# Long convolution and SwiGLU block: two LN2 norms offered to VectorE, more warming products, a new listed order

## The chip, the cores and the metric

The kernel runs on one core of a Trainium2 chip. The metric is the device time of one launch in microseconds (us). The kernel before took 261.85 us, the median of three runs (261.59 to 262.32).

## The reference

`S` = 2048 rows, `D` = 640 columns, `F` = 1728, inputs in bf16, batch 1. LayerNorm has no weights. The causal convolution over the whole sequence is written as a product of Fourier transforms padded to 2S.

```python
kv   = shift_conv(k, shift_k) * v              # four taps along the rows
y    = irfft2(rfft2(pad(kv)) * rfft2(pad(ssm_k)))[:S] + kv * ssm_D
h    = q + layernorm(q) * y
n    = layernorm(h)
out  = h + (silu(n @ w_gate) * (n @ w_up)) @ w_down
```

## The kernel before

**Tiling.** The sequence is cut into four blocks of 512 rows (four tiles of 128). The long convolution goes by blocks too: each block of `kv` (spectrum X) and of `ssm_k` (G, and H for the windows made of two neighbouring G) is taken to the frequency domain by products with a constant matrix on TensorE (L387, evicted in L376), X and H are multiplied and summed on VectorE (`mac`, L776 to L819, mostly L788, L816 and L817), and `inverse` goes back by products on TensorE (L955). `inverse` starts with an odd half (L898) and a low half (L901, or a DMA add in L906's place), needs the normalised rows of `ln1` (ScalarE, L882), multiplies them with the result (L979), adds them into h (L993, or a DMA that adds, issued by POOL in L291), takes the squares' sums for LN2 (ScalarE, L828) and ends with LN2's norm. `turn_h` normalises h (L882 on ScalarE, L879 on VectorE) and transposes it: block 0 on TensorE (L1015), the others by DMAs on SP's queue (L1008, four of them). The FFN of a block follows: products with gate and up weights (L1179, stretches of five), evictions (L1169, L1171, L1190), the product of the two (VectorE, L1173), and products with w_down (L1072), whose sums are added to h and stored (L1116, L1118 and L1120 for the last rows). Stages are named by block: X1, G2, m12, i1, t1, f1 and so on.

**norm.** `norm` turns the sums of a row into mean and 1/deviation, on 128x4 numbers. On VectorE it is ten short instructions that end in a cubic polynomial (L847 to L858, L864); on POOL it uses a power (L860 to L862). `ln1` gives its norm to POOL for all four blocks. LN2's norm goes to POOL in blocks 1 and 2 (`LN2POOL`) and to VectorE in blocks 0 and 3.

**The order.** The kernel doesn't issue in program order. `Plan` first collects all operations with their engine, reads and writes; `ORDER` (L76 to L115) then lists them by number, 940 entries, and each engine and each DMA queue runs what it is given in that order, first in, first out. An operation can have an alternative on another engine (an eviction on VectorE instead of ScalarE, an addition as a DMA, a load on POOL's queue instead of SP's); a negative number in the list selects it. Tiles come from a few pools of fixed size (`SLOTS`: four in PSUM, twelve big ones in SBUF, eight for spectra, five rows), so that an order also sets which buffer an operation waits for.

**The start.** While the first loads are under way TensorE runs products of ones with ones (`spin`, L1323 to L1331, `WARMUP` = 18, 16 and 16 of them) whose results nobody reads. Between them stand the transposes of the taps (`turn_taps`, L1336, and `turn_pairs`, L1353). The first real work is the transposes of block 0 of ssm_k (L485, loaded in L342) and of k (L628, loaded in L615), then the product for `kv` (L660). L1434 loads the last rows of w_down, 80 KB, twice.

Of the kernel before, what the change touches and what calls it, by code (L numbers as in the profile page):

```python
# [17 lines left out]
D = 640  # L18
# [30 lines left out]
ADDINV = ()  # L49
WHOLE3 = False  # L50
WARMUP = (18, 16, 16)
MERGE = ()
WIDE = ()
H1ACT = ()
# [19 lines left out]
TW = PAD + BLK  # L74
CUTS = ("X0", "G0", "m", "i")
ORDER = [  # L76
# [39 lines left out]
SLOTS = {'S': 8, 'big': 12, 'kT': 0, 'tT': 1, 'row': 5, 'sg': 0, 'co': 2, 'ps': 4, 'sm': 6}  # L116
HOME = {t: "big" for t in ("scr", "x", "ld", "t4", "hT", "wgu", "diag")} | {"o": "row", "ps_c": "ps", "ps_f": "ps"}
SPLIT = ((0,), (1,))
# [101 lines left out]
def kernel(ctx: ExitStack, tc: tile.TileContext, A_q, A_k, A_v, A_shift_k, A_ssm_k, A_ssm_D, B_x,  # L220
# [28 lines left out]
    def ap(b):  # L249
        if b.tag != "big":  # L250
            return b.ap if b.tag is None else place[b.tag][b.at]
        t = place["big"][b.at]
        return t if b.kind == "ld" else t.rearrange("p (k n) -> p k n", k=KT if b.kind in ("hT", "wgu") else 4 * KT if b.kind == "diag" else R)

    def pe(ns, fn, r, w, holds=(), late=338):
        op = plan.add("pe", ns, fn, r, w, holds)
        op.late = late
        return op
# [571 lines left out]

    def norm(s, v, mean=None, bias=False, rs=range(R)):

        def fused(out, a, scalar, b, op0, op1):
            if v is nc.vector:
                v.scalar_tensor_tensor(out, a, scalar, b, op0=op0, op1=op1)
            else:
                v.tensor_scalar(out, a, scalar, None, op0=op0)
                v.tensor_tensor(out, out, b, op=op1)
# [3 lines left out]
        def sm(s, i):  # L842
            return ap(s)[:, i, rs[0]:rs[-1] + 1:rs[1] - rs[0]]

        def go():
            if mean and plan_block in MERGEH:
                v.tensor_scalar(sm(s, 2), sm(s, 0), -1.0 / D, None, op0=ALU.mult)  # L847
            elif mean:
                fused(sm(s, 2), sm(s, 0), -1.0 / D, sm(mean, 2), ALU.mult, ALU.add)
            v.tensor_mul(sm(s, 6), sm(s, 2), sm(s, 2))  # L850
            if v is nc.vector:
                fused(sm(s, 3), sm(s, 1), EPS, sm(s, 6), ALU.add, ALU.subtract)
                v.tensor_scalar(sm(s, 4).bitcast(I32), sm(s, 3).bitcast(I32), -0.5, float(0x5F165000), op0=ALU.mult, op1=ALU.add)
                v.tensor_mul(sm(s, 6), sm(s, 4), sm(s, 4))
                v.scalar_tensor_tensor(sm(s, 6), sm(s, 6), -1.0, sm(s, 3), op0=ALU.mult, op1=ALU.mult)
# [6 lines left out]
                v.tensor_tensor(sm(s, 4), sm(s, 3), ap(root)[:, rs[0]:rs[-1] + 1:rs[1] - rs[0]], op=ALU.pow)  # L862
            if bias:
                v.tensor_mul(sm(s, 5), sm(s, 2), sm(s, 4))  # L864
        plan.add("dve" if v is nc.vector else "pool", 2190 if v is nc.vector else 7000 if mean else 5500, go, ([mean] if mean else []) + ([root] if v is nc.gpsimd else []), [s])

    def ln1(x):
        s = new("sm")
# [442 lines left out]
    def first(name):  # L1311
        plan.line(0, name)
# [33 lines left out]
    if TWOTAPS:  # L1346
# [4 lines left out]
        def turn_pairs():  # L1351
            for t in range(4):
                nc.tensor.matmul(ap(pt2)[:, 0, t * KT:(t + 1) * KT], ap(by_pair)[0:KT, t * P:(t + 1) * P], ap(ident)[0:KT, 0:KT], start=True, stop=True)  # L1353
        plan.name = "k0"
        pe(150, turn_pairs, [(by_pair, 0), ident], [pt2], (), 258)
        plan.name = "load"
        act(200, lambda: nc.scalar.copy(ap(taps2), ap(pt2)[:, 0, 0:4 * KT]), [pt2], [taps2])
        plan.add("pool", 350, lambda: nc.gpsimd.tensor_tensor(ap(by_pair)[:, 4 * P:4 * P + H2], ap(ident)[:, 0:H2], ap(ident)[:, H2:P], op=ALU.add), [ident], [(by_pair, 1)])
# [37 lines left out]
            ap(minus)[:, 2:4, :].rearrange("p a (c q) -> p a c q", c=4), ap(WI)[:, :, 1::2].rearrange("p c a q -> p a c q"), -1.0, None, op0=ALU.mult))  # L1396

    first("k0")
    k = turned_k(k, spun, table)
    again = spun  # L1400
    if not K0TURN:
# [116 lines left out]
```

## Time and profile before

| | before |
|---|---|
| median of 3 runs | 261.85 us |
| the profiled execution | 263.34 us |
| its span | 261.6 us |
| TensorE busy | 248.9 us, 95% |
| VectorE busy | 197.1 us, 75% |
| ScalarE busy | 184.9 us, 71% |
| POOL busy | 99.4 us, 38% |
| granted TensorE clock | 1.0 |

The span reaches from the first to the last instruction of the profiled execution; its own time, 263.34 us, is measured around it. In the profile PE is TensorE's products and PEld its weight loads, DVE is VectorE, ACT ScalarE, POOL GpSimd, SP SyncE; a q behind the name is the engine's queue of DMA issues and waits. A row of the timeline gives start, duration, engine, line, operation, output and inputs, and in square brackets the idle time ahead of it and what ended it.

### The profile page before, as it was taken

What the parts mean: (1) busy time and instruction counts of PE and PEld (TensorE: products, weight loads), DVE (VectorE), ACT (ScalarE), POOL (GpSimd) and SP (SyncE); (2) the same over time, 40 slices, a digit from 0 to 9 for tenths busy, and PEclk for the clock granted to TensorE, in tenths of its full rate; (3) what the DMA queues carried; (4) which work ended last, traced back from release to release, by engine and by line L of the source; (5) the groups of instructions that cost most, each with busy time, mean ns of one, the idle gap of its engine ahead of it and who ended that gap; (6) DMA issues with size and microseconds to landing.
All of it is one profiled execution on the core that took longest, in us unless ns stands there. A gap on an engine that the chain in (4) does not pass through costs nothing.

```text
span 261.6 us, 4550 instructions
## 1 busy us (share of the span) xinstructions
PE 248.9 (95%) x1738; PEld 149.6 (57%) x1738; DVE 197.1 (75%) x251; ACT 184.9 (71%) x308; POOL 99.4 (38%) x114
## 2 busy tenths in 40 slices
PE   7999998799997979999999999999999999999993
PEld 7985675554464437664456476544446754444662
DVE  4499999999996979999899999999999200102222
ACT  2799999999968789689679874866596332474300
POOL 7390700019995290144919621246960023000000
PEclk9999999999999999999999999999999999999999
DMA  6969999976938999699978959999996447000011
GB/s 213 386 126 263 252 291 338 202 220 122 345 89 158 195 190 259 118 168 221 296 123 136 338 128 171 174 238 199 207 285 189 82 93 97 6 0 3 0 34 66
DMA packets 65278, 45.91 MB, mean 175 GB/s; under 512 B 31029, under 2 KB 60410, under 8 KB 65258
## 3 DMA queue, kind: packets, MB, share of 16 engines
q1 hardware_dynamic: 59152, 32.51, 50.4%
q0 software_dynamic: 6096, 13.12, 26.7%
q8 instruction: 13, 0.21, 0.4%
q14 instruction: 7, 0.06, 0.1%
q10 hardware_dynamic: 10, 0.01, 0.0%
HBM read 29.56 MB, written 4.59 MB: 131 GB/s over the span
## 4 chain that ended last, share of the span: by engine, by line
PE 67%; ACT 9%; DVE 8%; POOL 7%; DMA 5%; issue 2%; DVEq 0%; POOLq 0%
PE ps L1179 31%; PE ps L1072 23%; POOL sm L850 6%; PE ps L387 5%; DMA big<-row 3%; PE ps L955 2%; ACT row L882 2%; DMA big<-in_A_ssm_k_dram 2%; PE ps L660 2%; ACT S L376 1%; DVE big L969 1%; ACT big L487 1%; ACT big L376 1%; DVE big L788 1%; DVE S L534 1%
## 5 line engine op out<-in xcount | busy, mean ns | idle before, releaser
L1179 PE MATMUL ps<-big,big 128*128 128x512 bf16 x540 | 119.8, 379 | 0.6 <-ACT co L1190 0.6
L1179 PEld LDWEIGHTS <-big 128*128 128x128 bf16 x540 | 52.6, 98 | 61.5 <-issue 1.1
L1072 PE MATMUL ps<-wd,tT 128*128 128x320 bf16 (+2 forms) x416 | 59.2, 299 | 0.5 <-ACT tT L1171 0.5
L1072 PEld LDWEIGHTS <-tT 128*128 128x128 bf16 x416 | 40.3, 98 | 17.7 <-issue 2.0
L1173 DVE TENSOR_TENSOR tT<-tT,co 128x2048 bf16<-128x2048 bf16 x12 | 14.7, 1223 | 38.9 <-ACT tT L1171 20.8
L387 PE MATMUL ps<-big,WF 128*128 128x320 bf16 x224 | 37.3, 298 | 2.7 <-ACT co L1169 1.2
L1169 ACT CAST co<-ps 128x1024 bf16<-128x1024 f32 x24 | 23.9, 1009 | 18.7 <-PE ps L1179 18.6
L816 DVE TENSOR_TENSOR big<-S,S 128x2560 bf16<-128x2560 bf16 x24 | 34.8, 1487 | 0.2
L817 DVE TENSOR_TENSOR S<-S,big 128x2560 bf16<-128x2560 bf16 x21 | 30.8, 1488 | 0.1
L387 PEld LDWEIGHTS <-WF 128*128 128x128 bf16 x224 | 21.3, 97 | 14.1 <-issue 4.9
L1171 ACT ACTIVATE tT<-ps 128x1024 bf16<-128x1024 f32 x24 | 24.3, 1027 | 3.8 <-PE ps L1179 3.5
L828 ACT ACTIVATE row<-big 128x640 bf16<-128x640 bf16 x32 | 23.5, 738 | 4.2 <-DMA big<-row 2.3
L1108 POOL DMA_DIRECT2D out_dram<-row x12 | 12.0, 1156 | 36.3 <-ACT row L1107 36.3
L882 ACT ACTIVATE row<-big,sm 128x640 bf16<-128x640 bf16 x23 | 19.7, 914 | 3.7 <-POOL sm L864 2.2
L850 POOL TENSOR_TENSOR sm<-sm 128x4 f32<-128x4 f32 x6 | 19.9, 3318 | 5.2 <-ACT row L871 5.0
L376 ACT CAST S<-ps 128x640 bf16<-128x640 f32 (+1 forms) x28 | 15.6, 613 | 2.0 <-PE ps L387 2.0
L376 ACT ACTIVATE big<-ps 128x640 bf16<-128x640 f32 (+1 forms) x27 | 15.5, 629 | 1.3 <-PE ps L387 1.1
L1107 ACT CAST row<-ps 128x640 bf16<-128x640 f32 x12 | 7.7, 700 | 10.8 <-PE ps L1072 10.8
L291 POOL DMA_DIRECT2D S<-big x6 | 7.2, 1206 | 19.0 <-DVE big L816 5.9
L955 PEld LDWEIGHTS <-WI 128*128 128x128 bf16 x96 | 9.4, 98 | 6.7 <-issue 1.7
L1050 POOL DMA_DIRECT2D big<-in_B_w_gate_dram x8 | 8.7, 1219 | 9.4 <-issue 6.8
L788 DVE TENSOR_TENSOR S<-S,S 128x2560 bf16<-128x2560 bf16 (+1 forms) x10 | 12.2, 1219 | 0.0
(112 smaller groups left out, 320.9 us busy)
## 6 DMA issues: line engine op xcount, KB each, us to landing
big<-in_B_w_up_dram SPq DMA_DIRECT2D x18, 320.0 KB, 5.6
big<-in_B_w_gate_dram SPq DMA_DIRECT2D x16, 320.0 KB, 5.5
big<-in_A_ssm_k_dram SPq DMA_DIRECT2D x4, 640.0 KB, 6.7
big<-in_A_q_dram SPq DMA_DIRECT2D x4, 640.0 KB, 5.5
big<-in_A_v_dram SPq DMA_DIRECT2D x4, 640.0 KB, 7.7
S<-big POOLq DMA_DIRECT2D x4, 640.0 KB, 6.3
big<-in_B_w_gate_dram POOLq DMA_DIRECT2D x8, 320.0 KB, 6.6
wd<-in_B_w_down_dram SPq DMA_DIRECT2D x1, 2080.0 KB, 11.9
```

Source lines behind the costliest of these rows:

```text
L376: (lambda: nc.scalar.activation(dst(), src(), ACT.Copy, scale=2.0)) if twice else (lambda: nc.scalar.copy(dst(), src())),
L387: nc.tensor.matmul(ap(ps)[:, h, 0:NH], w, ap(src)[:, r, h * NH:(h + 1) * NH], start=(first and i == 0), stop=(last and i == len(rs) - 1), ...
L788: return lambda: f(*(x() for x in args))
L816: dve(1490, lambda b=b, xs=xs, hs=hs: nc.vector.tensor_mul(flat2(b), X.part(xs), H.part(hs)), [X.at(xs), H.at(hs)], [b], [A.b])
L817: dve(1490, lambda b=b, dst=dst, f=f: f(A.part(dst), A.part(dst), flat2(b)), [b], [A.at(dst)])
L828: act(825, lambda r=r, junk=junk: nc.scalar.activation(ap(junk), ap(x)[:, r, :], ACT.Square, scale=D ** -0.5, accum_out=sm(s, 1)[:, r:r + ...
L850: v.tensor_mul(sm(s, 6), sm(s, 2), sm(s, 2))
L882: nc.scalar.activation(ap(row), ap(x)[:, r, :], ACT.Identity, bias=sm(s, 5)[:, r:r + 1], scale=sm(s, 4)[:, r:r + 1])
L1072: nc.tensor.matmul(to, t, w, skip_group_check=True, **flags)
L1169: act(1010, lambda ps=ps: nc.scalar.copy(ap(co)[:, at:at + 2, :], ap(ps)), src, [(co, gi % 2)])
L1171: act(1010, lambda ps=ps: nc.scalar.activation(ap(tT)[:, c:c + 2, :], ap(ps), ACT.Silu), src, [done(range(c, c + 2), ROWS)])
L1179: nc.tensor.matmul(ap(ps)[:, i, :], ap(w)[:, k, off:off + P], ap(hT)[:, k, :], start=(k == 0), stop=(k == KT - 1))
```

## The change

First, `norm`'s body takes its engine as an argument, and a norm that is planned on POOL gets the VectorE form as its alternative. Second, sixteen more warming products are planned: two groups of four ahead of `turn_pairs` (which waits for them) and two of four ahead of k's transposes. Third, the whole list `ORDER` is replaced (46 lines of it; numbers shift by two and then by four through the new operations).

```diff
+SPINS = (2, 2)
 ORDER = [
-    27, 28, 4, 1, 22, 0, 39, 2, 5, 6, 13, 7, 3, 14, 58, 10, 12, 56, 26, 8, 52, 15, 59, 57, 54, 24, 16, 11, 36, -54, 30, 55,
...
+    4, 15, 0, 1, 194, 30, 29, 2, 3, 14, 5, 18, 6, 13, 7, 16, 32, 58, 56, 17, 59, 9, 10, 24, 60, 33, 28, 8, 34, -58, 12, -62,
...
-        def fused(out, a, scalar, b, op0, op1):
+        def fused(v, out, a, scalar, b, op0, op1):
...
-        def go():
+        def go(v):
...
+        by_vector = 2190, lambda: go(nc.vector)
+        if v is nc.vector:
+            dve(*by_vector, [mean] if mean else [], [s])
+        else:
+            plan.add("pool", 7000 if mean else 5500, lambda: go(nc.gpsimd), ([mean] if mean else []) + [root], [s], (), ("dve",) + by_vector)
...
+        for _ in range(SPINS[0]):
+            spin(4)
+        some = plan.ops[len(plan.ops) - SPINS[0]:]
         plan.name = "k0"
-        pe(150, turn_pairs, [(by_pair, 0), ident], [pt2], (), 258)
+        pe(150, turn_pairs, [(by_pair, 0), ident], [pt2], (), 258).deps.update(some)
...
     first("k0")
+    for _ in range(SPINS[1]):
+        spin(4).deps.add(spun)
+        spun = plan.ops[-1]
     k = turned_k(k, spun, table)
```

What the new list selects and moves, as far as the prediction speaks of it:

- LN2's norms of blocks 1 and 2 run on VectorE (entries -305 and -526); the four norms of `ln1` stay on POOL.
- One of the two loads of L1434 is the first on SP's queue, ahead of all loads of block 0. Before, it was issued at 83 us, between weight loads.
- In block 0's t0 all four normalised rows (L879) are VectorE's, one behind the other; L534 no longer stands between them, and one L705 stands ahead of the norm.
- On POOL the DMA add of block 2's window (L531) stands ahead of `ln1`'s norm of block 1, and the low half of block 1's inverse becomes a DMA add behind it. Of block 1's h adds two go from a DMA to VectorE and one the other way.
- In f1 one load of gate weights follows the four L1008 turns of t1 on SP's queue; several other loads of f1, f2 and f3 change between SP's and POOL's queues.
- The last group of 128 rows of the output ends in a sum of 384 columns and one of 256, instead of two of them ahead and one of 640 at the end.
- Many evictions of G0, X0 and k0 change between ScalarE and VectorE, about as many one way as the other.

More of the change, by code (lines that the diff above doesn't have):

```diff
@@ L848, in go @@
             elif mean:
-                fused(sm(s, 2), sm(s, 0), -1.0 / D, sm(mean, 2), ALU.mult, ALU.add)
+                fused(v, sm(s, 2), sm(s, 0), -1.0 / D, sm(mean, 2), ALU.mult, ALU.add)
             v.tensor_mul(sm(s, 6), sm(s, 2), sm(s, 2))
             if v is nc.vector:
-                fused(sm(s, 3), sm(s, 1), EPS, sm(s, 6), ALU.add, ALU.subtract)
+                fused(v, sm(s, 3), sm(s, 1), EPS, sm(s, 6), ALU.add, ALU.subtract)
                 v.tensor_scalar(sm(s, 4).bitcast(I32), sm(s, 3).bitcast(I32), -0.5, float(0x5F165000), op0=ALU.mult, op1=ALU.add)
@@ L864, in go @@
                 v.tensor_mul(sm(s, 5), sm(s, 2), sm(s, 4))
-        plan.add("dve" if v is nc.vector else "pool", 2190 if v is nc.vector else 7000 if mean else 5500, go, ([mean] if mean else []) + ([root] if v is nc.gpsimd else []), [s])
+        by_vector = 2190, lambda: go(nc.vector)
[3 more added lines that the diff above has]
+            plan.add("pool", 7000 if mean else 5500, lambda: go(nc.gpsimd), ([mean] if mean else []) + [root], [s], (), ("dve",) + by_vector)
     def ln1(x):
```

77 rows, old and new, of the table ORDER are left out of this document.

## The prediction

> **What bounds the kernel now.** I read the page first, then the busy time by stage, then TensorE's waits, and last the timeline of each engine around the waits that are left.
>
> ```profile
> span 261.6 us, 4550 instructions
> ...
> PE 248.9 (95%) x1738; PEld 149.6 (57%) x1738; DVE 197.1 (75%) x251; ACT 184.9 (71%) x308; POOL 99.4 (38%) x114
> ...
> PE 67%; ACT 9%; DVE 8%; POOL 7%; DMA 5%; issue 2%; DVEq 0%; POOLq 0%
> ...
> big<-in_B_w_gate_dram SPq DMA_DIRECT2D x16, 320.0 KB, 5.5
> ```
>
> TensorE is busy for 248.9 of 261.6 us: whatever the new order does well, it can only win from 12.7 us. Two thirds of the chain that ended last are TensorE's own work, but 7% are POOL's, an engine that does little here. Where do the 12.7 us lie? The busy time by stage (window, its length, busy time of PE, PEld, DVE, ACT, POOL) answers:
>
> ```profile
> core 0: us, PE busy (x) PEld busy (x) DVE busy (x) ACT busy (x) POOL busy (x), PEclk, DMA share, GB/s
> 0.00:11.00 11.00, 9.67 (x101) 9.06 (x102) 5.25 (x23) 5.04 (x8) 5.06 (x15) 1.00 0.79 294
> 41.00:53.00 12.00, 9.34 (x91) 6.46 (x90) 11.61 (x25) 11.96 (x23) 0.26 (x1) 1.00 1.15 253
> 53.00:73.00 20.00, 20.00 (x118) 9.89 (x117) 20.00 (x16) 19.00 (x29) 14.69 (x3) 1.00 0.87 233
> 73.00:98.00 25.00, 21.15 (x152) 12.06 (x150) 20.87 (x24) 19.36 (x32) 16.29 (x19) 1.00 0.90 152
> 98.00:213.00 115.00, 114.93 (x740) 66.76 (x739) 104.15 (x115) 85.72 (x136) 45.49 (x47) 1.00 0.89 194
> 213.00:262.00 49.00, 44.65 (x251) 23.52 (x248) 7.58 (x10) 14.84 (x19) 4.42 (x5) 1.00 0.18 30
> ```
>
> TensorE's idle time is length less busy: 1.33 at the start, 2.66 in 41 to 53, 3.85 in 73 to 98, 0.07 in the 115 us of the three middle FFNs, 4.35 at the end. So the stages to look at are 41 to 53 (the norm and transposes of block 0) and 73 to 98 (the inverse of block 1). In the middle there is nothing to win, and 10.85 us of VectorE are free there (115 less 104.15).
>
> ```profile
> PE ps L955 <- ACT big L703: 1.5, 1, 1.5
> PE ps L387 <- ACT co L1169: 1.2, 1, 1.2
> PE ps L1015 <- DVE row L879: 1.0, 1, 1.0
> ...
> PE ps L1179 <- ACT co L1190: 0.6, 1, 0.6
> ```
>
> The 1.5 us is in block 1's inverse. Its cause stands two engines away (POOL, then VectorE, ScalarE, TensorE):
>
> ```profile
> 59.91 15.46 POOL L850 TENSOR_TENSOR sm<-sm 128x4 f32<-128x4 f32 x1
> 77.47 0.48 POOL L864 TENSOR_TENSOR sm<-sm 128x4 f32<-128x4 f32 x1
> 75.78 0.70 DVE L705 TENSOR_TENSOR big<-big,big 128x1024 bf16<-128x1024 bf16 x1 [0.46 <-ACT big L703]
> 77.98 0.92 ACT L882 ACTIVATE row<-big,sm 128x640 bf16<-128x640 bf16 x1 [2.23 <-POOL sm L864]
> 79.42 2.33 PE L955 MATMUL ps<-S,WI 128*128 128x320 bf16 x16 [1.50 <-ACT big L703]
> ```
>
> One multiplication of 128x4 numbers took POOL 15.46 us. VectorE was busy for all of 53 to 73 (20.00 of 20.00) and POOL came free at 75.37, just as VectorE paused (0.46 idle before 75.78). The last step of that norm ended at 77.95; ScalarE had stood 2.23 us for it, with the evictions of L703 queued behind, and TensorE lost 1.50. This is the ln1 norm of block 1, which stays on POOL after the change.
>
> **The norms of blocks 1 and 2.** What is moved is the other norm, of LN2 behind the inverse:
>
> ```profile
> 91.82 1.20 POOL L837 TENSOR_SCALAR sm<-sm 128x4 f32<-128x4 f32 x1
> 97.58 0.79 POOL L864 TENSOR_TENSOR sm<-sm 128x4 f32<-128x4 f32 x1
> 45.26 0.16 DVE L847 TENSOR_SCALAR sm<-sm 128x4 f32<-128x4 f32 x1
> 47.11 0.16 DVE L864 TENSOR_TENSOR sm<-sm 128x4 f32<-128x4 f32 x1
> ```
>
> On POOL block 1's took 91.82 to 98.37, 6.55 us; VectorE did a norm of block 0 in 45.26 to 47.27, 2.01 us. It comes 4.5 us sooner, yet its reader does not:
>
> ```profile
> 104.04 3.35 ACT L882 ACTIVATE row<-big,sm 128x640 bf16<-128x640 bf16 x4
> 106.24 5.18 SPq L1008 DMA_TRANSPOSE big<-row  x4
> 111.47 3.77 SPq L1050 DMA_DIRECT2D big<-in_B_w_up_dram  x3
> 115.86 2.32 PE L1179 MATMUL ps<-big,big 128*128 128x512 bf16 x10
> ```
>
> ScalarE reaches the four reads at 104.04, 5.7 us after the norm, because other work stands ahead of them. Only the list could bring them forward, and TensorE lacks no work there (0.07 idle). So the gain of the moved norms is **0**. Their cost is 2 x 2.01 = 4.0 us of VectorE, covered by its 10.85 free microseconds; without that cover it would be up to 4.0. The new list gives POOL's DMA adds some of VectorE's work (the low half at L906 for block 1, two products of the second mac) and takes back some h adds, so VectorE's sum hardly grows.
>
> The Trainium skill ("SBUF — State Buffer", section "Who interferes with whom") says that a GpSimd instruction which reads SBUF and a VectorE instruction with two SBUF inputs block one another for the whole instruction. The row at 91.82 fits, 1.20 us for 128x4 numbers; the row at 59.91 goes far beyond it, since it spans ten VectorE instructions and not one.
>
> **Block 1's inverse, 73 to 98.** The ln1 norm of block 1 stays on POOL. The list now has the DMA add of block 2's window (L531) ahead of it there, and behind it the DMA add of the low half (L906), which VectorE did before. Who waits: ScalarE's four L882, the evictions behind them, and, for L906, half of TensorE's inverse, which the list puts six stretches of five f0 products later (about 7 us of cover, at 1.16 a stretch by the row at 115.86). The group on the page:
>
> ```profile
> L850 POOL TENSOR_TENSOR sm<-sm 128x4 f32<-128x4 f32 x6 | 19.9, 3318 | 5.2 <-ACT row L871 5.0
> ```
>
> Without the long one the other five take (19.9 - 15.46) / 5 = 0.89 each. I take this usual case: the norm is done when the inverse starts, and 1.50 goes, and with it the 0.61 before L1179, whose eviction (L1190) stood behind the late ones: 2.11, with 0 as the other bound. The second cause in this stage is the h adds of block 1, which ran as DMAs:
>
> ```profile
> 92.00 0.74 ACT L828 ACTIVATE row<-big 128x640 bf16<-128x640 bf16 x1 [1.60 <-DMA big<-row]
> 95.27 0.43 PE L387 MATMUL ps<-big,WF 128*128 128x320 bf16 x2 [1.24 <-ACT co L1169]
> ```
>
> Two of these adds move to VectorE, one goes the other way. What is left of the stage's 3.85 after 2.11 is 1.74; a gain of 0 and one of 1.74 are the bounds, and I take half, 0.85, since one add of the three that matter still goes by DMA. Together **-2.95**.
>
> **Start.** Sixteen warming products are added (4 x 4), and on SP the 80 KB load of L1434 moves from the middle of the kernel to the head:
>
> ```profile
> 0.83 2.08 PE L1329 MATMUL ps<-const-bfloat16-1.0 128*128 128x128 bf16 x18 [0.83 <-PEq L1502]
> 5.71 2.32 PE L485 MATMUL ps<-ident,big 128*128 128x128 bf16 x20 [0.35 <-DMA big<-in_A_ssm_k_dram]
> 11.20 1.00 PE L660 MATMUL ps<-big,T 128*128 128x128 bf16 x15
> L1434 SPq DMA_DIRECT2D wd<-in_B_w_down_dram x2: 1236/1286/1335, 12.6 to 83.3; - x2
> ```
>
> The products take 116 ns at first (2.08 / 18 and 2.32 / 20) and 67 at 11.20 (1.00 / 15). L1434 holds SP for 1.29, so the first load, for which TensorE already waits at 5.71, comes up to 1.3 later; at least 0.27, its 80 KB at the 294 GB/s of the stage. If the added products brought the fast rate forward to 5.71, the 40 products of L485 and L628 would take 40 x (116 - 67) ns = 2.0 less. So the start moves by -1.7 (all fast, 0.27 late) to +1.3 (none fast, 1.3 late); with both in full it is -0.7. I take **+0.5**, between the last two and nearer to the later one, since the products of L628 wait for a load too and the fast ones then only wait longer.
>
> The Trainium skill ("TensorE: Matmul & The Clock Gate", section "Part 1: The HAM clock gate") has TensorE at half clock until it was busy through a window of about 3.4 us. The trace agrees with a switch somewhere between 5.71 and 11.20; if four more small bursts fill the gaps before 5.71, the rule speaks for the -1.7, the warming rival below.
>
> **Block 0's transposes, 41 to 53.**
>
> ```profile
> 47.79 0.44 DVE L879 TENSOR_SCALAR row<-big,sm 128x640 bf16<-128x640 bf16 x1
> 48.15 1.48 DVE L534 TENSOR_TENSOR S<-S,S 128x2560 bf16<-128x2560 bf16 x1
> 49.55 0.80 DVE L879 TENSOR_SCALAR row<-big,sm 128x640 bf16<-128x640 bf16 x2
> ```
>
> The new list runs the four reads of block 0 (L879) in a row: L534 (1.48) goes from between them, one L705 (0.70 by the row at 75.78) comes ahead of the norm and the fourth read (0.44) comes from ScalarE: -1.48 + 0.70 + 0.44 = **-0.34**. If the wait of 1.0 at L1015 has other causes too, it is 0; the two waits there allow no more than the stage's 2.66.
>
> **First weights of f1.** The order sends one 320 KB gate load through SP directly behind the four turns of L1008. Behind it on SP stand four more weight loads of f1. The turns hold SP until 111.42; the load lands 5.5 later (the DMA row on the page), at 116.9; TensorE starts at 115.86 and needs it some 1.2 later (half of the row's 2.32), at 117.1. So it is just in time. A wait of 0 and of 4.9 (the issue time of all four turns, which the load has ahead of it) are the bounds; I take **+0.6**.
>
> **End.** Now the last addition is 640 wide; in the new list it is one of 384:
>
> ```profile
> 257.69 0.82 DVE L1116 TENSOR_TENSOR row<-ps,big 128x640 bf16<-128x640 f32 x1 [1.46 <-PE ps L1072]
> L1118 DVE TENSOR_TENSOR row<-ps,big x2: 425/486/548, 252.6 to 252.9; 128x256 bf16<-128x256 f32 x1, 128x384 bf16<-128x384 f32 x1
> ```
>
> 0.82 - 0.55 = **-0.3**. **Elsewhere** a list of 940 entries can only lose where 0.07 is idle: **+0.6**, the size of one wait in the list above; the bounds are 0 and 3.85, what the worst stage loses now.
>
> **Sum.** +0.5 - 0.34 - 2.95 + 0.6 - 0.3 + 0.6 = -1.9. The profiled execution took 263.34 (span 261.6 and 1.7 around it), the median of three runs is 261.85. I take the difference from the median: **260.0**.
>
> **Rivals.**
> *POOL starves again* (262.1). VectorE is still without a pause from 53 to 73 (20.00 of 20.00), the norm's first instruction ends at its first pause, and the 2.11 stays: -1.9 + 2.1 = +0.2. Every microsecond by which that pause comes later than 75.37 would be one more, since ScalarE stands at L882 in the meantime. For it: the DMA add and the mac are again its neighbours. Against it: one of six such instructions was long.
> *The f1 load is late by all of the turns* (264.3). Place: SP between L1008 and the gate load. Price 4.9 in place of 0.6, so -1.9 - 0.6 + 4.9 = +2.4. It ends slower once the wait passes 2.5 us, as the rest of the sum is -2.5. For it: SP issues in order, and the margin worked out above is 0.2. Against it: the page's landing time of 5.5 is a median under the same traffic.
> *The middle loses as much as 73 to 98 does now* (263.2): 3.85 in place of 0.6, so -1.9 - 0.6 + 3.85 = +1.35. For it: with 0.07 idle nothing can be won there, and a list that differs in hundreds of places has many chances of a wait. Against it: ScalarE has 29 us to spare there and VectorE 11.
> *The warming wins all* (257.8): -1.7 in place of +0.5, so -4.1. For it: TensorE has nothing else to do before 5.71. Against it: 1.3 us of SP stand ahead of every load it needs.
> That the moved norms, the change's first word, do nothing for the time is no rival but part of the forecast.
>
> **How the numbers follow.** Forecast 0.34, warming 0.12, starved 0.20, f1 load 0.22, middle 0.12. Faster by over 0.3% (0.8 us, about what a measurement of this kernel can tell) are the first two, 0.46. The starved case is at +0.2: 0.14 of it within 0.3%, and 0.06 slower, for the later pause. Slower 0.06 + 0.22 + 0.12 = 0.40. The likeliest one's own range is 258.9 to 261.0. The range for all reaches from near the warming case, 257.9, to the f1 case, 264.3.
>
> **What would show it.** L850 of block 1 at about 1.3 us, and no wait of ScalarE's L882 behind L864, if the inverse is right; L955 without a wait. LN2's norm of blocks 1 and 2 on VectorE in 2.0 us each with f1 and f2 starting when they did. The first L485 at about 6.5 to 7 and L660 at 11.7. TensorE's first f1 product and the gate load's landing within 1 us of each other. The forecast is wrong if L850 on POOL is long again, if f1 waits over 2.5 us for a load, or if 98 to 213 shows more than 1 us idle.

## The result and the profile after

The changed kernel takes 276.5 us (median of four runs, 272.92 to 280.25), the kernel before 262.09 beside it: ratio 1.0393, 95% interval 1.0278 to 1.0508. It is slower by 4% and more, where 0.7% faster was forecast. Two of the four executions took 280 us and two 273; the ratio goes by the shorter ones alone, as the comparison leaves runs well above the fastest out, and the profiled execution is a longer one, 280.25 us with a span of 278.4. What sets them apart is told below as far as it was seen.

The page of the changed kernel (its lines have moved by 2 behind the list and by 6 behind `norm`; L852 is L850 of before, L1185 is L1179):

```profile
span 278.4 us, 4585 instructions
...
PE 254.8 (92%) x1754; PEld 152.3 (55%) x1754; DVE 197.6 (71%) x274; ACT 185.0 (66%) x306; POOL 93.4 (34%) x101
...
PE 56%; POOL 11%; DVE 11%; ACT 10%; DMA 7%; issue 3%; SPq 0%; POOLq 0%; DVEq 0%
...
L852 POOL TENSOR_TENSOR sm<-sm 128x4 f32<-128x4 f32 x4 | 24.1, 6024 | 1.9 <-ACT row L877 1.9
```

TensorE has 5.9 us more of busy time for the same products, apart from sixteen small ones, and 10.9 us more of idle time (23.6 against 12.7). VectorE and ScalarE work as long as before. POOL's share of the chain rose from 7 to 11% although POOL does less. The busy time by stage, same columns as in the prediction, tells where:

```profile
41.00:53.00 12.00, 10.18 (x87) 6.83 (x85) 11.58 (x29) 11.36 (x23) 0.22 (x1) 1.00 1.02 223
53.00:73.00 20.00, 20.00 (x100) 9.60 (x99) 19.89 (x16) 18.60 (x30) 9.89 (x8) 1.00 1.00 230
73.00:98.00 25.00, 24.55 (x195) 15.10 (x194) 24.58 (x28) 24.74 (x38) 4.49 (x5) 1.00 1.02 194
98.00:213.00 115.00, 99.83 (x594) 54.37 (x593) 93.83 (x107) 74.67 (x116) 53.82 (x37) 0.94 0.83 171
```

In 73 to 98 TensorE's idle time fell from 3.85 to 0.45, in 41 to 53 from 2.66 to 1.82: there the new list does what was forecast. In 98 to 213 it rose from 0.07 to 15.17, and the granted clock fell to 0.94. Two waits make up most of it (TensorE's waits of the changed kernel; behind the colon the total in us, the number and the longest):

```profile
PE ps L389 <- ACT row L1113: 8.5, 1, 8.5
PE ps L1185 <- ACT tT L1177: 5.8, 1, 5.8
PE ps L961 <- ACT tT L1177: 1.0, 1, 1.0
```

**The wait of 5.8 us**, followed back in the timeline:

```profile
115.15 16.52 POOL L852 TENSOR_TENSOR sm<-sm 128x4 f32<-128x4 f32 x1 [1.18 <-ACT row L877]
114.42 2.89 DVE L819 TENSOR_TENSOR S<-S,big 128x2560 bf16<-128x2560 bf16 x2
...
130.05 1.55 DVE L941 TENSOR_TENSOR S<-big 128x1280 bf16<-128x1280 bf16 x2
133.72 2.54 ACT L888 ACTIVATE row<-big,sm 128x640 bf16<-128x640 bf16 x3 [6.43 <-POOL sm L866]
137.22 3.60 PE L1185 MATMUL ps<-big,big 128*128 128x512 bf16 x10 [5.79 <-ACT tT L1177]
```

This is `ln1`'s norm of block 2, on POOL as before. VectorE ran without a pause from before 114.42 to 131.60, and the multiplication of 128x4 numbers ended at 131.67, in the pause. ScalarE stood 6.43 us for the norm, with FFN evictions queued behind, and TensorE stood for these. It is what the prediction describes for block 1, a block later. In the kernel before the same instruction of block 2 took 0.34 us:

```profile
121.46 0.34 POOL L850 TENSOR_TENSOR sm<-sm 128x4 f32<-128x4 f32 x1 [5.05 <-ACT row L871]
```

**The wait of 8.5 us** is in block 2's t2:

```profile
161.76 5.17 SPq L1014 DMA_TRANSPOSE big<-row  x3
172.70 0.74 ACT L830 ACTIVATE row<-big 128x640 bf16<-128x640 bf16 x1 [6.38 <-DMA big<-row]
176.21 0.74 ACT L877 ACTIVATE row<-big 128x640 bf16<-128x640 bf16 x1 [2.69 <-DMA big<-row]
168.62 1.26 PE L1078 MATMUL ps<-wd,tT 128*128 128x320 bf16 x8
178.39 0.69 PE L389 MATMUL ps<-big,WF 128*128 128x320 bf16 x2 [8.51 <-ACT row L1113]
178.87 2.34 PE L1078 MATMUL ps<-wd,tT 128*128 128x320 bf16 x8
```

ScalarE wants a row buffer for its next statistics; the others of the five are held by normalised rows on their way through a transposing DMA. A transposing DMA usually lands 2.6 us behind its issue; here the slowest took 12.2:

```profile
DMA to landing us min/median/max: 2.6/2.6/12.2
```

Behind ScalarE stand the evictions of L1113, so no PSUM buffer comes free and TensorE stands. The rows at 168.62 and 178.87 show a second cost: the same eight products take 1.26 us before the wait and 2.34 behind it. Behind the 5.79 us wait ten products of L1185 took 3.60, where 2.32 is usual. Half rate behind the two waits makes up some 4.1 of the 5.9 us by which busy time grew, an estimate: each slowed row in the trace (these two and the three or four behind them) less the time of the same row at the full rate.

### The profile page after: what moved, and what is told of

The parts are those of the page before. It is cut to its first block, busy times and chain, and to the rows that moved or that the text cites. A ratio compares the mean times of both kernels' runs of the same rounds, so it can differ in the third digit from the quotient of the medians.

```text
span 278.4 us, 4585 instructions
## 1 busy us (share of the span) xinstructions
PE 254.8 (92%) x1754; PEld 152.3 (55%) x1754; DVE 197.6 (71%) x274; ACT 185.0 (66%) x306; POOL 93.4 (34%) x101
## 4 chain that ended last, share of the span: by engine, by line
PE 56%; POOL 11%; DVE 11%; ACT 10%; DMA 7%; issue 3%; SPq 0%; POOLq 0%; DVEq 0%
PE ps L1185 27%; PE ps L1078 19%; POOL sm L852 7%; DMA big<-row 5%; PE ps L389 4%; PE ps L961 2%; ACT row L830 2%; DVE S L790 2%; DMA big<-in_A_ssm_k_dram 2%; ACT big L378 2%; DVE big L818 2%; PE ps L717 1%; ACT S L378 1%; ACT row L888 1%; ACT row L877 1%
## 5 line engine op out<-in xcount | busy, mean ns | idle before, releaser
L1185 PE MATMUL ps<-big,big 128*128 128x512 bf16 x540 | 122.2, 384 | 6.2 <-ACT tT L1177 5.8
L1185 PEld LDWEIGHTS <-big 128*128 128x128 bf16 x540 | 53.3, 99 | 68.7 <-issue 9.1
L1078 PE MATMUL ps<-wd,tT 128*128 128x320 bf16 (+2 forms) x416 | 61.4, 302 | 0.0
L1078 PEld LDWEIGHTS <-tT 128*128 128x128 bf16 x416 | 40.7, 99 | 18.3 <-issue 1.8
L389 PE MATMUL ps<-big,WF 128*128 128x320 bf16 x224 | 38.6, 303 | 10.8 <-ACT row L1113 8.5
L1179 DVE TENSOR_TENSOR tT<-tT,co 128x2048 bf16<-128x2048 bf16 x12 | 14.7, 1221 | 31.9 <-ACT tT L1177 25.0
L389 PEld LDWEIGHTS <-WF 128*128 128x128 bf16 x224 | 21.7, 98 | 22.5 <-issue 13.5
L830 ACT ACTIVATE row<-big 128x640 bf16<-128x640 bf16 x32 | 23.9, 750 | 7.2 <-DMA big<-row 6.4
L819 DVE TENSOR_TENSOR S<-S,big 128x2560 bf16<-128x2560 bf16 x18 | 26.2, 1485 | 0.0
L852 POOL TENSOR_TENSOR sm<-sm 128x4 f32<-128x4 f32 x4 | 24.1, 6024 | 1.9 <-ACT row L877 1.9
L378 ACT ACTIVATE big<-ps 128x640 bf16<-128x640 f32 (+1 forms) x29 | 16.5, 616 | 2.6 <-PE ps L389 2.4
L293 POOL DMA_DIRECT2D S<-big x8 | 9.6, 1194 | 25.5 <-DVE S L819 10.3
L985 DVE SCALAR_TENSOR_TENSOR row<-row,ps 128x640 bf16<-128x640 bf16 x12 | 9.7, 817 | 8.6 <-ACT row L888 5.2
L1056 POOL DMA_DIRECT2D big<-in_B_w_up_dram x10 | 10.7, 1072 | 12.1 <-issue 11.6
L877 ACT ACTIVATE row<-big 128x640 bf16<-128x640 bf16 x16 | 12.3, 770 | 2.7 <-DMA big<-row 2.7
L961 PEld LDWEIGHTS <-WI 128*128 128x128 bf16 x96 | 9.2, 98 | 6.2 <-issue 1.8
```

The source lines that it names most:

```text
L378: (lambda: nc.scalar.activation(dst(), src(), ACT.Copy, scale=2.0)) if twice else (lambda: nc.scalar.copy(dst(), src())),
L389: nc.tensor.matmul(ap(ps)[:, h, 0:NH], w, ap(src)[:, r, h * NH:(h + 1) * NH], start=(first and i == 0), stop=(last and i == len(rs) - 1), ...
L819: dve(1490, lambda b=b, dst=dst, f=f: f(A.part(dst), A.part(dst), flat2(b)), [b], [A.at(dst)])
L830: act(825, lambda r=r, junk=junk: nc.scalar.activation(ap(junk), ap(x)[:, r, :], ACT.Square, scale=D ** -0.5, accum_out=sm(s, 1)[:, r:r + ...
L877: act(820, lambda r=r, junk=junk: nc.scalar.activation(ap(junk), ap(x)[:, r, :], ACT.Identity, scale=-1.0 / D, accum_out=sm(s, 2)[:, r:r + ...
L1078: nc.tensor.matmul(to, t, w, skip_group_check=True, **flags)
```

## The experiments

Ratios are to runs of the kernel before on the same chip in the same session, whose median lay between 262.1 and 263.0; edits are to the list by the changed kernel's numbers, unless another is named (-499 selects the alternative of entry 498, and so on). Rows have the line numbers of their own kernel: in the three runs with the list of before, L829, L851, L960 and L1174 are L828, L850, L955 and L1169 of before.

**The change once more.**

> The changed kernel once more, unedited. Its four executions so far were 280.25, 272.93, 280.06 and 272.92, so it has two times, 7.1 us apart. In the profiled one (280.25) TensorE waited 5.79 us once and 8.51 us once, and ran at half rate for a while behind each. Theory P (the 7.1 us are the POOL norm of ln1 in block 2, which took 16.5 us there in one instruction): executions fall at 273 or 280 again, and one at 273 shows that instruction at 1 to 10 us with a wait of TensorE under 1 us, and the 8.51 us wait unchanged. Theory Q (the 7.1 us are the late transposes of t2): one at 273 shows the 5.79 us wait unchanged and the 8.51 us wait under 2 us.

Executions 279.26, 275.46, 278.31 and 273.66; ratio 1.0476 (1.0407 to 1.0545). The profiled one, 279.26, waits 5.8 us at L1185 as before, but 4.7 at L389 instead of 8.5, and 3.2 at L717 for a DMA that the first profile doesn't show. No trace of this list with both faults is of an execution at 273. So which wait makes the two times isn't settled by these two traces; what varies between them is the late transposes, not POOL's norm (5.8 in both). A third trace, below in `copy_first`, points the same way.

**One part of each wait taken away.**

```diff
n2_norm_dve:          498 -> -499            (ln1's norm of block 2 on VectorE)
loads_behind_turns:   ..., 531, 765, -783, -773, ...   (three f2 loads behind t2's last turn)
both:                 the two together
```

> The changed kernel with ln1's norm of block 2 on VectorE (one entry of the list takes its alternative, at its place). Theory P: no 16.5 us instruction on POOL, the wait of 5.79 us of TensorE and the half rate behind it (10 products in 3.60 instead of 2.32 us) go, 7.1 us in all, and all executions are near 273. Rival (ScalarE's evictions in block 2's inverse are late for another reason): the wait stays over 4 us and both times stay.

> The changed kernel with three 320 KB weight loads of f2 moved in the list behind the last of t2's four transposing DMAs (one on SP's queue, two on POOL's). Theory T (the transposes landed 11 and 12 us after their issue since these loads shared the DMA engines, and held the row buffers that ScalarE waited for): the transposes land within 4 us, ScalarE's waits of 6.38 and 2.69 us and TensorE's of 8.51 us go, and with them the half rate behind it, some 10 us: 263 and 270. Rival (the transposes are late for another reason, or f2's weights are now what is late): the wait stays or moves to f2, change under 3 us.

> Both edits. If P and T both hold, the sum: 280.1 - 7.1 - 10 = 263 or a little below, one time only. If either is wrong, its part stays: 270 or 273.

| run | median us | ratio to before, 95% |
|---|---|---|
| the change once more | 276.89 | 1.0476 (1.0407 to 1.0545) |
| n2_norm_dve | 269.99 | 1.0235 (1.0156 to 1.0314) |
| loads_behind_turns | 269.91 | 1.0315 (1.0248 to 1.0382) |
| both | 263.81 | 1.0045 (1.0009 to 1.0081) |

Each edit takes its own wait and leaves the other. With the norm on VectorE the 5.8 is gone and 4.1 us at L389 are left (waits of n2_norm_dve):

```profile
PE ps L389 <- ACT row L1113: 4.1, 1, 4.1
```

With the loads behind the turns no transposing DMA took over 4.1 us and L389 no longer waits for L1113, while the 5.8 stays (loads_behind_turns):

```profile
PE ps L1185 <- ACT tT L1177: 5.8, 1, 5.8
...
DMA to landing us min/median/max: 2.6/2.8/4.1
```

By the medians each is worth about 7 us and both 13.1, all but 1.0 of the loss to the kernel before in that session (262.81). So the two waits, with the half rate behind them, are nearly all of the loss. The misses in the expectations are of size. `n2_norm_dve` fell to between 266.99 and 272.87 instead of 273, as the late transposes it leaves vary (the wait at L389 was 8.5, 4.7 and 4.1 us in three traces). `loads_behind_turns` came at 269.01 to 272.6 and not at two times. `both` was expected at one time only: seven of its nine executions took 261.50 to 264.46, and two 266.51 and 270.46, at a granted clock of 0.987 and 0.981 where the seven have 0.994 to 1.0. What was left in those two no trace shows.

With the norm out of the way f1 shows another wait, which the 5.8 us had hidden: weights that land late, 1.7 us in `n2_norm_dve` and 2.3 in `both`:

```profile
130.68 2.33 PE L1185 MATMUL ps<-big,big 128*128 128x512 bf16 x10 [2.27 <-DMA big<-in_B_w_up_dram]
```

**Which instruction starves.** In `norm`, ahead of POOL's first multiplication:

```diff
+            if v is nc.gpsimd and not mean:
+                v.tensor_copy(sm(s, 6), sm(s, 2))
             v.tensor_mul(sm(s, 6), sm(s, 2), sm(s, 2))
```

> The changed kernel with one small copy of 128x4 numbers ahead of POOL's first multiplication in each ln1 norm. It tells what in block 2's norm takes 16.5 us. Theory F (POOL's first access in a stretch in which VectorE's instructions follow one another without a pause waits until the pause): the copy takes 15 to 17 us and the multiplication about 1. Theory M (it is this multiplication, whatever stands ahead): the copy takes under 2 us and the multiplication 14 or more. Either way the time stays at 273 to 280.

```profile
117.90 16.52 POOL L853 COPY sm<-sm 128x4 f32<-128x4 f32 x1 [1.16 <-ACT row L879]
134.50 0.19 POOL L854 TENSOR_TENSOR sm<-sm 128x4 f32<-128x4 f32 x1
```

The one execution took 275.28 us. Of the two theories F is right in that the 16.5 us fall on what comes first, and the multiplication then takes 0.19. (That every first access waits for a pause, as F has it, does not hold: see block 1 below.)

The same trace bears on the two times of the changed kernel. Its wait behind the norm is 6.0 us, its wait for the late transposes only 2.3, and behind that one the eight products keep their full rate (L1115 and L1080 are L1113 and L1078 of the change):

```profile
PE ps L389 <- ACT row L1115: 2.3, 1, 2.3
...
176.35 1.25 PE L1080 MATMUL ps<-wd,tT 128*128 128x320 bf16 x8
```

So from 8.5 over 4.7 to 2.3 us at L389 the executions took 280.25, 279.26 and 275.28, with the norm's wait nearly the same. The mean granted clock, on record for every execution, fits: 0.975 in those at 278.31 to 280.25, 0.981 at 275.28 and 275.46, 0.987 in the three at 273, and 0.980 to 0.987 in `loads_behind_turns`, where the norm's wait stands alone. The shorter time is thus most likely the one in which the transposes are late by less; a trace of one at 273 is lacking.

**The prediction's parts, each alone in the list of before.**

```diff
before_ln2_norms:   300 -> -301, 521 -> -522, SPINS = (0, 0)    (numbers of before)
before_ln1_norm1:   277 -> -278, SPINS = (0, 0)                 (numbers of before)
before_spins:       the list of before, with the four groups of warming products
```

> The kernel before with its own list, and only LN2's norms of blocks 1 and 2 on VectorE, no added warming products: the part that the change names first, alone. The prediction's term: 0, as ScalarE reaches the readers long behind the norm (104.0 against 98.4 us in block 1): within 0.8 us of before, with the rows of f1 and f2 starting where they did. Rival (VectorE has no cover): up to 4.0 us slower, with TensorE's waits behind VectorE's evictions or products.

Median 263.85, ratio 1.0045 (1.0007 to 1.0082): somewhat slower, by 1.2 us where 0.8 was the expected limit. ScalarE's order is the old one, and two short waits are new in the middle FFNs, where VectorE's work now comes later (before_ln2_norms):

```profile
PE ps L960 <- DVE S L925: 0.7, 2, 0.6
98.00:213.00 115.00, 113.89 (x725) 65.86 (x731) 105.83 (x132) 85.19 (x136) 38.62 (x39) 1.00 0.85 192
```

1.11 us are idle there, 0.07 before. The cover that the prediction named was nearly but not quite enough.

> The kernel before with its own list, and only ln1's norm of block 1 (15.46 us for one instruction on POOL) on VectorE, at its place in the list. The prediction's term for that wait: 2.1 us, so 2.1 us faster, TensorE's wait of 1.5 us at the inverse gone. Rival: VectorE is full in that stage, its norm of 2.0 us pushes back the low half that TensorE's inverse reads, and the wait stays under another name: within 0.8 us of before.

Median 259.22, ratio 0.9871 (0.9839 to 0.9904), 3 us faster than before and the fastest kernel of all. VectorE does the norm between two mac products, and TensorE's wait of 1.5 is 0.7 (its rival's wait, at VectorE's own product). The 1.24 of the h adds goes as well (before_ln1_norm1):

```profile
66.24 0.15 DVE L851 TENSOR_TENSOR sm<-sm 128x4 f32<-128x4 f32 x1
...
79.65 2.35 PE L960 MATMUL ps<-S,WI 128*128 128x320 bf16 x16 [0.74 <-DVE S L906]
```

> The kernel before with its own list, and only the sixteen warming products added (four groups of four). The first ssm_k load is where it was on SP's queue. Prediction's range for the start with no later load: 0 (no earlier fast rate) to -2.0. If the fast rate comes by the first transposes, L485 shows 67 ns a product instead of 116 and the kv products start up to 1 us earlier; but the load of k lands at 7.6 us in the kernel before, so I expect 0.3 us faster, within noise.

Median 264.48, ratio 1.0070 (1.0046 to 1.0094): slower. The first twenty transposes take 1.47 us instead of 2.32, and kv's products start at 10.94 instead of 11.20, yet TensorE waits 2.82 instead of 1.24 behind block 1's h adds (before_spins):

```profile
94.81 0.74 ACT L829 ACTIVATE row<-big 128x640 bf16<-128x640 bf16 x1 [2.10 <-DMA big<-row]
96.59 0.43 PE L388 MATMUL ps<-big,WF 128*128 128x320 bf16 x2 [2.82 <-ACT co L1174]
```

Whether that loss belongs to the products was asked with the norm out of the way:

> The list of before with ln1's norm of block 1 on VectorE (259.2 us) and the sixteen warming products. With the products alone the list of before was 2.1 us slower, by a longer wait behind block 1's h adds (DMAs that landed at 94.8 instead of 93.5 us). With the norm on VectorE these adds go out earlier and nothing waited behind them. If that wait was the whole loss: 258.9 to 259.2, the earlier start kept or hidden. If the products cost by themselves: 261.

Median 259.88, ratio 0.9893 (0.9855 to 0.9930), against 0.9871 without the products: no difference that these intervals show. The wait behind the adds is not among its waits. So the loss most likely was that wait, 1.58 of some 2 us by the two traces; that it was open only because the starved norm had pushed the adds late fits this, but no run shows it alone.

**The list mended.** `both`, and ln1's norm of block 3 on VectorE (its 1.0 us at L961 is the third row of the waits above), and the load of L1434 back behind its old neighbour:

```diff
727 -> -728;   ..., 622, 194, ...   instead of   4, 15, 0, 1, 194, 30, ...
```

> The changed kernel with both ln1 norms that starved on VectorE (blocks 2 and 3), the three f2 loads behind t2's turns, and the L1434 load back to its old neighbours on SP's queue. The run with the first two edits for block 2 took 263.5 to 264.5 mostly. Now the wait of 1.3 us at block 3's inverse goes and the first load lands 1.1 us earlier: 261 to 262, level with before or just under. Rival (the start doesn't recover and the weights of f1 stay 2.3 us late): 263.5.

> The mended list with the L1434 load at the head of SP's queue, as the change has it. The first ssm_k load landed at 5.75 us with L1434 back and at 6.5 to 6.9 with it ahead, and kv's products started at 10.41 against 11.0 to 12.4. If the whole start is carried to the end: 0.6 to 1.3 us slower than 261.3. If the stages behind the start have slack for it: under 0.3.

Mended 261.30, ratio 0.9946 (0.9918 to 0.9974); with L1434 at the head of the queue 262.05, ratio 0.9949 (0.9913 to 0.9985). The load's place makes no difference to the end that is seen, though the first ssm_k load lands at 5.75 with it back and at 6.5 to 6.9 with it first. `mended_l1434_first` differs from `both` in the third norm alone, and its ratio is lower by 1%, some 2.5 us. But that is not all the norm's: its wait was 1.3 us in `both`, and 1.6 us more went because f1's late weights cost 0.7 instead of 2.3, some 50 us ahead of that norm; the two runs are also of two sessions on two chips. The list without its faults is thus a little faster than before, 0.5%.

**The change's first part undone in the mended list.**

```diff
mended_ln2_pool:   -305 -> 304, -526 -> 525   (LN2's norms back on POOL)
```

> The mended list (ln1's norms of blocks 2 and 3 on VectorE, three f2 loads behind t2's turns, L1434 back; 261.3 us) with LN2's norms of blocks 1 and 2 back on POOL, at their places in the list: the change's first part undone in its own list. Theory N (this part costs VectorE 4 us that are nearly covered and gains nothing): within 1 us of 261.3. Theory G (in the new list the readers are close behind the norm, so that POOL's 6.5 to 7 us, or a starved instruction, are exposed): 264 or more, with a wait of ScalarE behind the norm in t1 or t2.

Median 265.20, ratio 1.0074 (1.0033 to 1.0116): 1.3% slower than mended. So in this list the norms on VectorE are worth over 3 us, but not in the way that theory G says: ScalarE reads block 1's norm at the same time in both. The timeline of mended_ln2_pool, and below it the mended one's:

```profile
101.69 0.20 POOL L866 TENSOR_TENSOR sm<-sm 128x4 f32<-128x4 f32 x1
102.21 1.26 POOL L293 DMA_DIRECT2D S<-big  x1 [0.33 <-issue]
101.92 3.36 ACT L888 ACTIVATE row<-big,sm 128x640 bf16<-128x640 bf16 x4
110.78 1.32 ACT L1113 CAST row<-ps 128x640 bf16<-128x640 f32 x2 [1.91 <-DMA big<-row]
111.53 0.70 PE L389 MATMUL ps<-big,WF 128*128 128x320 bf16 x4 [1.76 <-ACT row L1113]
...
DMA to landing us min/median/max: 2.6/4.7/7.8
```

```profile
98.28 1.19 POOL L293 DMA_DIRECT2D S<-big  x1 [2.90 <-DVE tail L1208]
101.98 3.36 ACT L888 ACTIVATE row<-big,sm 128x640 bf16<-128x640 bf16 x4
...
DMA to landing us min/median/max: 2.6/3.5/5.1
```

A DMA add of the spectra is queued on POOL behind the norm. With the norm on POOL it goes out at 102.21, just ahead of the turns, which land up to 7.8 us behind their issue, hold the row buffers, and stop L1113 and TensorE: it looks like the 8.5 us wait in small. Without the norm ahead of it the add goes out at 98.28, and the turns land within 5.1. In block 2 it is alike: the add goes out at 151.78 instead of 147.89, and TensorE waits some 1.0 us twice. In 98 to 213 TensorE is idle for 3.93 us with the norms on POOL and 0.76 without. That the add delays the turns is read from these two traces; no run moves the add alone.

## Why the prediction was wrong

The forecast was 260.0 in a range of 257.9 to 264.3. What failed is one step (1) and one omission (2); together they made the term **Elsewhere**, +0.6, into 15.1 us of idle time and the half rate behind it.

1. **The starved norm was priced in one block only.** "I take this usual case: the norm is done when the inverse starts": that came true for block 1, where the stage's idle time fell by 3.40 (forecast 2.95), and the kernel of before with that norm on VectorE gained 3 us (term: 2.1). But three more ln1 norms stay on POOL, and the list was read for VectorE's pauses around one. In block 2 the new list puts the norm in 16.5 us of VectorE without a pause, worth 7 us by `n2_norm_dve`; in block 3 the same instruction took 4.85 us and TensorE waited 1.0. The rival *POOL starves again* was the right mechanism with the wrong place, and its price of 2.1 came from block 1, where TensorE lost 1.50 to it against 5.79 here.

   In block 1 the step was lucky. VectorE was as full there as the rival's condition says (19.89 of the 20.00 us from 53 to 73), yet POOL's first multiplication took 2.37 us and ended between two VectorE instructions, without a pause of more than 0.1. The prediction had only the count of one long instruction in six for that (the changed kernel):

```profile
61.64 1.49 DVE L424 TENSOR_TENSOR S<-big,S 128x2560 bf16<-128x2560 bf16 x1
62.40 2.37 POOL L852 TENSOR_TENSOR sm<-sm 128x4 f32<-128x4 f32 x1
63.23 4.29 DVE L818 TENSOR_TENSOR big<-S,S 128x2560 bf16<-128x2560 bf16 x3
```

2. **The transposes' place among DMAs was not looked at for t2.** The f1 rival asked what is queued behind t1's turns on SP. Its load was not late: TensorE started f1 at 111.82 without a wait. (A later load of f1 was, by 1.7 and 2.3 us, in `n2_norm_dve` and `both`; in the change the wait for the norm hid it.) What decided is what shares the DMA engines with t2's turns, and the row buffers that these hold: 8.5, 4.7, 4.1 and 2.3 us in four traces. Who waits for a buffer that a DMA holds was asked for loads alone.
3. **Elsewhere, +0.6,** had 3.85 as its bound, from the worst stage of before. What a bad order costs in a stage is not bounded by what the old order lost in another: it lost 15.1 there. The range ended too low for that reason.
4. **"The gain of the moved norms is 0"** holds in the old list (1.2 us lost there, of VectorE's order), and fails in the new one by over 3 us: what is behind the norm on POOL's queue, a DMA add, was not counted (by the two traces, as said, not by a run of its own).
5. **Start, +0.5.** In the profiled execution kv's products start at 12.38, 1.2 later; in the six other traces with L1434 first at 10.99 to 11.53, -0.2 to +0.3. At the head of the queue the load held SP for 0.58 us, not 1.29. The range of the term held, and the end does not depend on it (the ratios 0.9946 and 0.9949).
6. **Block 0, -0.34:** idle in 41 to 53 fell by 0.84, right in sign. **End, -0.3:** from TensorE's last product to the end of the span it is 3.1 against 4.0, right in sign.

One reading of the profile was off by one: the row at 59.91 spans eleven VectorE instructions, not ten.

The Trainium skill ("TensorE: Matmul & The Clock Gate", section "Part 1: The HAM clock gate") says that the array falls back to half its rate when it was idle for a window of some 3.4 us. The trace agrees: 1.26 became 2.34 for eight products behind 8.51 us of idle time, and 2.32 became 3.60 behind 5.79, while behind 2.28 (`copy_first`) the eight products took 1.25; the rule belonged in the sum for the middle too, since it makes a long wait dearer by a fifth or more.

## What to carry to other kernels

A small instruction on POOL can wait for VectorE's next pause (16.5 us here, though not each one does), so read for each one, in the new order, how long VectorE runs without a pause from the moment its inputs are there; do it for all blocks, not the one that showed the fault, and price that length as the bound. A transposing DMA holds its source buffer until it lands, so list what shares the DMA engines with it, and who is next for that buffer. Where a list is replaced as a whole, the idle time of the old one is no bound on what the new one loses.

## What the runs showed of the hardware

One POOL instruction on 128x4 numbers took 15.46 us in the old list and 16.52 in the new, whichever operation it was (a multiplication, a copy), and in the two cases whose VectorE rows are shown it ended in VectorE's first pause; other POOL instructions got through at the next boundary of two VectorE instructions, in 1.2 to 1.3 us, and the same first instruction of a norm at a boundary without a pause in 2.37 (block 1 of the changed kernel). The Trainium skill ("SBUF — State Buffer", section "Who interferes with whom") has the loser blocked for the whole of one instruction; here it was blocked over more than ten in a row. Why the first of a norm's instructions is passed over for so long in one block and not in another, no run here tells.

The same sixteen warming products brought the fast rate to the first transposes in all but one of the traces with the new list (15 products in 1.03 us, at 6.52 to 6.84 with L1434 first and at 5.79 to 5.80 with it back; in the first profile of the change 1.79). The same kernel can thus start with or without it.
